# Two neighbouring attention heads on one tile: 64 partitions each, one softmax, one load and store for both

## The chip, the core and the metric

The kernel runs on one core of one Trainium2 chip. TensorE (PE) multiplies and transposes, VectorE (DVE), ScalarE (ACT) and GpSimd (POOL) compute elementwise, and SyncE (SP) issues most of the DMAs. The time is the device time of one launch in microseconds (us). The span in a profile runs from the first to the last instruction and is somewhat shorter.

## The reference

One decoding step, forward and backward. An attention block with 32 heads reads one token x (640 wide) and a cache of 4096 keys and values per head, each 128 wide. A dense block with the Mish activation (640 to 1728 to 640) reads another token, a constant. A sigmoid gate g of x mixes the two:

```python
q = (x @ wq).reshape(B, Sq, H, Dh).transpose(0, 2, 1, 3)
scores = jnp.einsum("bhqd,bhkd->bhqk", q, k_cache) * (Dh ** -0.5)
p = _softmax(scores, axis=-1)
o = jnp.einsum("bhqk,bhkd->bhqd", p, v_cache)
a = o.transpose(0, 2, 1, 3).reshape(B, Sq, H * Dh) @ wo
out = g * a + (1 - g) * b
```

The kernel returns the output and the gradients by x, both caches, wq, wo, w1, b1, w2 and the gate's weights. Inputs and outputs are bfloat16. For each head the gradients of the caches are outer products over the 4096 positions: dV = p times the row dO, and dK = ds times the row q, where ds = p (dO.v - sum of p dO.v). Each cache and each cache gradient has 33.5 MB, so nearly all bytes are those of the four: 134 MB of the 164.56 MB that the DMA engines move.

## The kernel before

**Tiling.** A head's K is one tile Kn of 128 partitions with J = 32 positions on each, 128 values a position: 8 KB on a partition, contiguous in memory, 1 MB in all. V, dK and dV lie the same way. Heads go in groups of G = 4, which share the rows q and dO and the columns of wq and rows of wo that belong to them. The pool kv_in holds four K and four V tiles, outs four output tiles.

**One head, in steps** (names of the helpers and of the tiles in the profile):

- `load_k`, `load_v`: one DMA each, issued by SP.
- `k_pe(h, c)`, `v_pe(h, c)`, c from 0 to 3 (line 541): four transposes on TensorE into one PSUM tile tr (three buffers). `ev` (line 550): ScalarE copies the oldest tr into T.
- `k_rows`, `v_rows` (line 564): eight matmuls each, scores q.k and products dO.v, all into one PSUM tile rw. `rw_cp` (line 575): ScalarE copies rw. `x_tr` (line 581): four transposes bring them to positions on partitions, tile x; two columns of it are the scores and the products.
- `maxes` (lines 587, 589): largest score of each partition. `softmax` (lines 593, 595): a transpose and a maximum give the largest of all. `exps` (line 601): ScalarE's exponential with its sum. `pjs` (line 605), `zd_mm` (line 609): the two sums, over the partitions by a matmul with ones. `probs` (lines 613 to 619): p and ds, each value four times beside itself.
- `dq_o` (line 657): 16 matmuls of ds and p with K and V, into rw again; they are the last readers of the head's K and V. `dqo_red` (line 665) adds up their diagonals one head later.
- `dv_out(h, k)`, `dk_out(h, k)`, k = 0 and 1 (line 624): VectorE writes an outer product of half a tile; after the second half SP stores the tile (line 642).

**Order.** The order of every engine's instructions is that in which the helpers are called: the kernel's pools run under a manual schedule, and each engine takes its instructions in order. The loop over heads at line 772 interleaves head h's softmax with the transposes of head h + 1 and the first two K tiles of head h + 2. The load of head h + 4 is called after dq_o(h), because it takes that head's buffer; thus a load is called two heads before its first transpose:

```python
k_pe(h + 2, 0)
dq_o(h)
v_rows(h + 1)
rw_cp(h + 1)
```

**Between the heads.** At the first head of a group (hh = 0) the previous group's gradients are finished: `f_diag`, `f_bc`, `l_pe`, `f_dwo` (dwo, on ScalarE), and `f_dx` with `f_dwq` (lines 392, 402, five column chunks, on VectorE), two chunks there and three at hh = 1. The next group's rows are made over hh = 1 to 3: `w_pe` (transposes of wo), `g_q`, `g_do`, and `g_qcol`, `g_qpair`, `g_qpair_cp` and their dO counterparts, which bring q and dO into the columns of qz and doz. The dense block's work waits in the list mq and is called in portions by `mlp_some(budget)`, whose costs are the numbers in m_cost (line 674); `dw2_some` adds ScalarE's dw2 copies.

Of the kernel before, what the change touches and what calls it, by code (L numbers as in the profile page):

```python
# [16 lines left out]
def kernel(  # L17
# [24 lines left out]
    nc = tc.nc  # L42
# [5 lines left out]
    J = Sk // P  # L48
# [16 lines left out]
    NTB = J // TB  # L65
    JH = J // 2

    Kv = A_k_cache.rearrange("b h (p j) d -> (b h) p j d", p=P)
    Vv = A_v_cache.rearrange("b h (p j) d -> (b h) p j d", p=P)
    dKv = out_2.rearrange("b h (p j) d -> (b h) p j d", p=P)  # L70
    dVv = out_3.rearrange("b h (p j) d -> (b h) p j d", p=P)
# [20 lines left out]
    KBUFS, VBUFS = 4, 4  # L92
    kv_in = ctx.enter_context(tc.tile_pool(name="kv_in", bufs=KBUFS))
    kvT = ctx.enter_context(tc.tile_pool(name="kvT", bufs=1))
    outs = ctx.enter_context(tc.tile_pool(name="outs", bufs=4))
# [10 lines left out]
    def load_k(h):  # L106
        if h < H:
            kts[h] = kv_in.tile([P, J, Dh], BF16, name="Kn", tag="Kn")
            nc.sync.dma_start(kts[h][:], Kv[h])

    def load_v(h):
        if h < H:
            vts[h] = kv_in.tile([P, J, Dh], BF16, name="Vn", tag="Vn", bufs=VBUFS)
            nc.sync.dma_start(vts[h][:], Vv[h])
# [24 lines left out]
    load_k(0)  # L139
    load_wqp(0)  # L140
    load_wo(0)
    load_v(0)
    load_k(1)
    load_v(1)
    load_k(2)
    load_wo(1)
    load_v(2)
    load_k(3)
    load_v(3)
    w1_sb = const.tile([P, RC, F], BF16, name="w1_sb")  # L150
    nc.sync.dma_start(w1_sb[:], w1_v)
    w2_sb = const.tile([P, FCN, D], BF16, name="w2_sb")
# [17 lines left out]
    nc.vector.reduce_sum(half[:], ident_bf[:].rearrange("p (a k) -> p a k", a=2), axis=AX.X)  # L170
    unzip = const.tile([P, 2, P], BF16, name="unzip")
# [45 lines left out]
    p4b, ds4b = [], []  # L217
    qz = const.tile([P, G, 2, 2, 16], BF16, name="qz")
    doz = const.tile([P, G, 2, 2, 16], BF16, name="doz")
    nc.gpsimd.memset(qz[:], 0.0)  # L220
    nc.gpsimd.memset(doz[:], 0.0)
    for i in range(3):
        for lst, nm in ((p4b, "p4"), (ds4b, "ds4")):
            lst.append(const.tile([P, J * 4], BF16, name=f"{nm}{i}"))
            nc.gpsimd.memset(lst[-1][:], 0.0)
# [3 lines left out]
    def g_new(g):  # L229
        groups[g] = dict(  # L230
            q_row=grp_sb.tile([P, GD], BF16, name="q_row", tag="q_row", bufs=1),
            qs_row=grp_sb.tile([P, GD], BF16, name="qs_row", tag="qs_row"),
            do_row=grp_sb.tile([P, GD], BF16, name="do_row", tag="do_row"),
            dqo=grp_sb.tile([P, 2, G], F32, name="dqo", tag="dqo"),
        )

    def g_q(g):
        gp = groups[g]
        ps = grp([P, GD], F32, "q_ps")
        for rc in range(RC):  # L240
            nc.tensor.matmul(ps[:], lhsT=x_col_bf[:, rc:rc + 1].to_broadcast([P, P]),  # L241
                             rhs=wqs[g][:, rc, :], start=(rc == 0), stop=(rc == RC - 1))
        nc.scalar.copy(gp["q_row"][:], ps[:])
# [5 lines left out]
    def col_mm(row):  # L249
        ps = grp([P, G], F32, "col_ps")  # L250
        for hh in range(G):
            nc.tensor.matmul(ps[:, hh:hh + 1], lhsT=row[0:1, hh * Dh:(hh + 1) * Dh], rhs=ones_bf[0:1, 0:1],
                             start=True, stop=True)
        col = small.tile([P, G], BF16, name="col", tag="col", bufs=2)
        nc.vector.tensor_copy(col[:], ps[:])
        return col
# [7 lines left out]
    def pair_cp(z, ps, at):  # L264
        for par in range(2):
            nc.vector.tensor_tensor(z[:, :, par, :, at],
                                    ps[:, par, :].unsqueeze(2).to_broadcast([P, G, 2]),
                                    half[:].unsqueeze(1).to_broadcast([P, G, 2]), ALU.mult)
# [7 lines left out]
    def g_qpair_cp(g):  # L276
        pair_cp(qz, groups[g].pop("pair"), 4)
# [7 lines left out]
    def g_dopair_cp(g):  # L285
        pair_cp(doz, groups[g].pop("pair"), 5)

    def g_do(g):
        gp = groups[g]
        ps = grp([P, GD], F32, "do_ps")  # L290
        T = wT.pop(("o", g))
        for c in range(RC):
            nc.tensor.matmul(ps[:], lhsT=da_col[:, c:c + 1].to_broadcast([P, P]),  # L293
                             rhs=T[:, c * G:(c + 1) * G, :].rearrange("p t k -> p (t k)"),
                             start=(c == 0), stop=(c == RC - 1))
# [235 lines left out]
    KT, VT, dgms, es, zds, p4s, ds4s = {}, {}, {}, {}, {}, {}, {}  # L531
# [3 lines left out]
    rw_sb, xs, sd = {}, {}, {}  # L535

    def tr_pe(h, tiles, T, c):
        tp = tr_ps.tile([P, TB // 2, P], F32, name="tr", tag="tr")
        words = tiles[h][:, c * TB:(c + 1) * TB, :].rearrange("p a b -> p (a b)").bitcast(F32)
        for t in range(TB // 2):  # L540
            nc.tensor.transpose(tp[:, t, :], words[:, t * P:(t + 1) * P], ident_f[:])  # L541
        trq.append(lambda: kv_ev(tp, T, h, c))

    def ev():
        trq.pop(0)()

    def kv_ev(tp, T, h, c):
        if c == 0:
            T[h] = kvT.tile([P, J // 2, P], F32, name="T", tag="T")
        nc.scalar.copy(T[h][:, (3 - c) * (TB // 2):(4 - c) * (TB // 2), :], tp[:])  # L550

    def k_pe(h, c):
        if h < H:
            tr_pe(h, kts, KT, c)

    def v_pe(h, c):
        if h < H:
            tr_pe(h, vts, VT, c)

    def rows_mm(T, z, first):  # L560
        Tb = T[:].rearrange("p k r -> p (k r)").bitcast(BF16).rearrange("p (t c r a) -> p c a t r", t=4, c=4, a=2)
        for par in range(2):
            for c in range(4):
                nc.tensor.matmul(rw[32 * c:32 * (c + 1), :], lhsT=z[:, par, :, :].rearrange("p m u -> p (m u)"),  # L564
                                 rhs=Tb[:, c, par, :, :], start=first and par == 0, stop=not first and par == 1)

    def k_rows(h):
        rows_mm(KT.pop(h), qz[:, h % G], True)

    def v_rows(h):  # L570
        rows_mm(VT.pop(h), doz[:, h % G], False)

    def rw_cp(h):
        rw_sb[h] = small.tile([P, 4, P], F32, name="rw_sb", tag="rw_sb", bufs=1)
        nc.scalar.copy(rw_sb[h][:].rearrange("p t r -> p (t r)"), rw[:])  # L575

    def x_tr(h):
        t = rw_sb.pop(h)
        xs[h] = s_ps.tile([P, 4, P], F32, name="x", tag="x")
        for j in range(4):  # L580
            nc.tensor.transpose(xs[h][:, 3 - j, :], t[:, j, :], ident_f[:])  # L581
        v = xs[h][:].rearrange("p t r -> p (t r)").rearrange("p (j u) -> p j u", u=16)
        sd[h] = (v[:, :, 4], v[:, :, 5])

    def maxes(h):
        m32 = small.tile([P, 1], F32, name="m32", tag="m32")
        nc.vector.tensor_reduce(m32[:], sd[h][0], axis=AX.X, op=ALU.max)
        dgms[h] = small.tile([P, 1], F32, name="m_s", tag="m_s")
        nc.vector.tensor_scalar(dgms[h][:], m32[:], scale, None, ALU.mult)  # L589

    def softmax(h):
        mx = s_ps.tile([P, P + 2], F32, name="mx", tag="mx")
        nc.tensor.transpose(mx[:, 0:P], dgms.pop(h)[:].to_broadcast([P, P]), ident_f[:])  # L593
        negM = small.tile([P, 1], F32, name="negM", tag="negM")
        nc.vector.tensor_reduce(negM[:], mx[:, 0:P], axis=AX.X, op=ALU.max, negate=True)
        return mx, negM

    def exps(h, negM):
        es[h] = small.tile([P, J], BF16, name="e_bf", tag="e_bf")
        zds[h] = small.tile([P, 2], F32, name="zd", tag="zd")  # L600
        nc.scalar.activation(es[h][:], sd[h][0], ACT.Exp, bias=negM[:], scale=scale, accum_out=zds[h][:, 0:1])  # L601

    def pjs(h):
        pj = small.tile([P, J], F32, name="pj", tag="pj", bufs=2)
        nc.vector.scalar_tensor_tensor(pj[:], in0=sd[h][1], scalar=1.0, in1=es[h][:],  # L605
                                       op0=ALU.mult, op1=ALU.mult, accum_out=zds[h][:, 1:2])

    def zd_mm(h, mx):
        nc.tensor.matmul(mx[:, P:P + 2], lhsT=ones_f[:], rhs=zds[h][:], start=True, stop=True)  # L609

    def probs(h, mx):
# [4 lines left out]
        p4s[h] = p4b[h % 3][:, 0:J * 4].rearrange("p (j t) -> p j t", t=4)  # L616
        nc.vector.tensor_scalar(p4s[h], es.pop(h)[:].unsqueeze(2).to_broadcast([P, J, 4]), rz[:], None, ALU.mult)
        ds4s[h] = ds4b[h % 3][:, 0:J * 4].rearrange("p (j t) -> p j t", t=4)
        nc.vector.scalar_tensor_tensor(ds4s[h], in0=sd.pop(h)[1].unsqueeze(2).to_broadcast([P, J, 4]),  # L619
                                       scalar=negD[:], in1=p4s[h], op0=ALU.add, op1=ALU.mult)  # L620
        zds.pop(h)
# [9 lines left out]
    def out_half(w, h, dst, col4, row, k):  # L631
        hh = h % G
        if k == 0:
            if w == "k" and H - KBUFS <= h < H - 1:
                o_t[w, h] = kv_in.tile([P, J, Dh], BF16, name="Kn", tag="Kn")
            elif w == "v" and h > H - VBUFS:
                o_t[w, h] = kv_in.tile([P, J, Dh], BF16, name="Vn", tag="Vn", bufs=VBUFS)
            else:
                o_t[w, h] = outs.tile([P, J, Dh], BF16, name="o_sb", tag="o_sb")
        outer(o_t[w, h], col4, row[:, hh * Dh:(hh + 1) * Dh], k * JH, (k + 1) * JH)  # L640
        if k == 1:
# [339 lines left out]
```

## Time and profile before

| | |
|---|---|
| median of 3 runs | 401.09 us (400.48 to 402.11) |
| profiled execution | 399.99 us |
| its span | 398.3 us |
| bytes moved | 164.56 MB, 82.44 MB read and 82.44 MB written |
| heads' transfers | 64 loads and 64 stores of 1024 KB |
| median from issue to landing, K load | 16.6 us |
| TensorE clock granted, mean | 0.937 |

The page's first part gives the busy time of the engines, its second the share in 40 slices of the span, the fourth the chain of work that ended last. A row of the waits names the waiting instruction, what released it, the total in us, how often, and the longest. A row of the timeline gives the start, the duration, the engine, the line, the operation with its tiles, and in brackets the idle time before it. For DMA the digits are the mean busy share of 16 engines in tenths.

### The profile page before, as it was taken

To read this page: it belongs to the slowest core of one execution; us is meant where nothing else is said; L and a number is where in the kernel's file an instruction comes from. 1 tells how busy PE (TensorE), PEld (TensorE's weight loads), DVE (VectorE), ACT (ScalarE), POOL (GpSimd) and SP (SyncE) were. 2 spreads that over 40 slices of the span, in tenths; PEclk is the share of its full clock that TensorE was granted. 3 is DMA by queue.
4 is the path that set the end of the run, shared out by engine and by line. 5 is a ranking of instruction groups with operands and counts; after the bars stand their busy time and mean duration, and the time that the engine had idled before them with its cause. 6 is when DMAs were issued, how large, how long until landed. Compare 5 with 4: busy or idle time off the path is not lost.

```text
span 398.3 us, 7758 instructions
## 1 busy us (share of the span) xinstructions
PE 298.7 (75%) x2950; PEld 201.4 (51%) x2950; DVE 288.6 (72%) x823; ACT 232.8 (58%) x468; POOL 29.3 (7%) x54
## 2 busy tenths in 40 slices
PE   2779979777898984875887876968786888578550
PEld 1556647554565663554564553645454555356320
DVE  3216647969688875778898974697897987488880
ACT  2356756853677562763567677575777666285420
POOL 9300023000000000000000070000000000010001
PEclk9999999998999998999999999869999999698955
DMA  7999999999999999999999999999999999999996
GB/s 270 421 426 406 426 419 423 420 418 425 423 423 425 413 408 428 425 415 425 423 423 425 421 424 421 426 412 425 425 423 427 421 427 418 423 432 421 386 419 267
DMA packets 28469, 164.56 MB, mean 413 GB/s; under 512 B 3383, under 2 KB 3384, under 8 KB 11832
## 3 DMA queue, kind: packets, MB, share of 16 engines
q1 hardware_dynamic: 27312, 159.62, 96.6%
q0 software_dynamic: 1088, 4.44, 2.7%
q8 instruction: 23, 0.38, 0.4%
q14 instruction: 14, 0.11, 0.1%
q10 hardware_dynamic: 32, 0.01, 0.0%
HBM read 82.44 MB, written 82.44 MB: 414 GB/s over the span
## 4 chain that ended last, share of the span: by engine, by line
DMA 46%; DVE 25%; PE 20%; ACT 5%; issue 2%; POOL 0%; POOLq 0%; SPq 0%; DVEq 0%; ACTq 0%
DMA out_dram<-o_sb 44%; DVE o_sb L624 10%; PE tr L541 7%; DVE junk L392 4%; PE rw L657 3%; PE rw L564 2%; DVE wq_p L402 2%; DMA wq_p<-in_A_wq_dram 2%; PE x L581 1%; ACT rw_sb L575 1%; ACT do_row L296 1%; PE do_ps L293 1%; PE tr L354 1%; PE h_ps L436 1%; PE q_ps L241 1%
## 5 line engine op out<-in xcount | busy, mean ns | idle before, releaser
L550 ACT COPY T<-tr 128x512 f32<-128x512 f32 x256 | 138.0, 595 | 53.8 <-PE tr L541 38.8
L624 DVE TENSOR_TENSOR o_sb<-qs_row,ds 128x2048 bf16<-128x2048 bf16 x58 | 70.8, 1221 | 37.5 <-DMA out_dram<-o_sb 37.5
L541 PE MATMUL tr<-ident_f,Kn 128*128 128x128 f32 x512 | 84.3, 292 | 5.8 <-DMA Kn<-in_A_k_cache_dram 5.8
L541 PE MATMUL tr<-ident_f,Vn 128*128 128x128 f32 x512 | 82.7, 294 | 7.2 <-ACT T L550 6.4
L541 PEld LDWEIGHTS tr<-ident_f,Vn 128*128 128x128 f32 x512 | 61.4, 151 | 26.9 <-PE tr L541 11.5
L541 PEld LDWEIGHTS tr<-ident_f,Kn 128*128 128x128 f32 x512 | 60.5, 148 | 23.2 <-PE rw L657 13.5
L624 DVE TENSOR_TENSOR o_sb<-do_row,p 128x2048 bf16<-128x2048 bf16 x58 | 68.9, 1229 | 0.0
L575 ACT COPY rw_sb<-rw 128x512 f32<-128x512 f32 x33 | 19.3, 586 | 48.3 <-PE rw L564 46.1
L657 PE MATMUL rw<-Kn,ds 128*4 128x512 bf16 x256 | 36.2, 408 | 4.1 <-DVE ds L619 3.8
L657 PE MATMUL rw<-Vn,p 128*4 128x512 bf16 x256 | 36.2, 408 | 0.0
L593 PE MATMUL mx<-ident_f,m_s 128*128 128x128 f32 x32 | 10.2, 318 | 30.8 <-DVE m_s L589 30.7
L581 PE MATMUL x<-ident_f,rw_sb 128*128 128x128 f32 x132 | 22.1, 291 | 4.6 <-ACT rw_sb L575 1.4
L392 DVE SCALAR_TENSOR_TENSOR junk<-wq_p,dq_bc 128x512 bf16<-128x512 bf16 x35 | 23.9, 683 | 0.0
L609 PE MATMUL mx<-zd,ones_f 128*128 128x2 f32 x64 | 10.7, 237 | 17.6 <-DVE pj L605 17.5
L601 ACT ACTIVATE e_bf<-x,negM 128x32 bf16<-128x32 f32 x32 | 9.4, 293 | 23.0 <-DVE dqo L665 23.0
L593 PEld LDWEIGHTS mx<-ident_f,m_s 128*128 128x128 f32 x32 | 4.4, 139 | 35.2 <-DVE m_s L589 35.2
L410 ACT ACTIVATE wo_g<-da_bc,o 128x640 bf16<-128x640 bf16 x28 | 20.9, 818 | 1.0 <-PE ax_ps L380 1.0
L564 PE MATMUL rw<-T,qz 128*32 128x512 bf16 x256 | 21.4, 412 | 0.0
L581 PEld LDWEIGHTS x<-ident_f,rw_sb 128*128 128x128 f32 x132 | 14.1, 143 | 13.4 <-ACT rw_sb L575 13.4
L564 PE MATMUL rw<-T,doz 128*32 128x512 bf16 x256 | 20.3, 392 | 0.8 <-ACT T L550 0.8
L609 PEld LDWEIGHTS mx<-zd,ones_f 128*128 128x128 f32 x64 | 10.1, 198 | 20.9 <-DVE pj L605 18.2
L657 PEld LDWEIGHTS <-ds 128*4 128x4 bf16 x256 | 9.2, 86 | 20.1 <-DVE ds L619 9.3
(181 smaller groups left out, 381.5 us busy)
## 6 DMA issues: line engine op xcount, KB each, us to landing
out_dram<-o_sb SPq DMA_DIRECT2D x58, 1024.0 KB, 16.4
Kn<-in_A_k_cache_dram SPq DMA_DIRECT2D x32, 1024.0 KB, 16.6
Vn<-in_A_v_cache_dram SPq DMA_DIRECT2D x32, 1024.0 KB, 18.1
wq_p<-in_A_wq_dram SPq DMA_DIRECT2D x4, 1280.0 KB, 14.2
wo_g<-in_A_wo_dram SPq DMA_DIRECT2D x8, 640.0 KB, 17.3
out_dram<-wo_g SPq DMA_DIRECT2D x8, 640.0 KB, 16.5
out_dram<-wq_p SPq DMA_DIRECT2D x4, 1280.0 KB, 9.5
out_dram<-Kn SPq DMA_DIRECT2D x3, 1024.0 KB, 7.8
```

Source lines behind the costliest of these rows:

```text
L392: nc.vector.scalar_tensor_tensor(jq[:], in0=wqs[g][:, c, :], scalar=1.0, in1=groups[g]["dq_bc"][:], op0=ALU.mult, op1=ALU.mult, accum_out= ...
L410: nc.scalar.activation(wos[g][:, hh, :], da_bc[:], ACT.Copy, scale=groups[g]["o4"][:, hh:hh + 1])
L541: nc.tensor.transpose(tp[:, t, :], words[:, t * P:(t + 1) * P], ident_f[:])
L550: nc.scalar.copy(T[h][:, (3 - c) * (TB // 2):(4 - c) * (TB // 2), :], tp[:])
L564: nc.tensor.matmul(rw[32 * c:32 * (c + 1), :], lhsT=z[:, par, :, :].rearrange("p m u -> p (m u)"), rhs=Tb[:, c, par, :, :], start=first an ...
L575: nc.scalar.copy(rw_sb[h][:].rearrange("p t r -> p (t r)"), rw[:])
L581: nc.tensor.transpose(xs[h][:, 3 - j, :], t[:, j, :], ident_f[:])
L593: nc.tensor.transpose(mx[:, 0:P], dgms.pop(h)[:].to_broadcast([P, P]), ident_f[:])
L601: nc.scalar.activation(es[h][:], sd[h][0], ACT.Exp, bias=negM[:], scale=scale, accum_out=zds[h][:, 0:1])
L609: nc.tensor.matmul(mx[:, P:P + 2], lhsT=ones_f[:], rhs=zds[h][:], start=True, stop=True)
L624: nc.vector.tensor_tensor(dst[:, a:b, :].rearrange("p j (k t) -> p j k t", t=4), row.rearrange("p (k t) -> p k t", t=4).unsqueeze(1).to_br ...
L657: nc.tensor.matmul(rw[32 * c:32 * c + 4, :], lhsT=c4[:, 4 * jb:4 * jb + 16].rearrange("p (j t) -> p t j", t=4)[:, 0, :], rhs=N[:, jb:jb + ...
```

## The change

Two neighbouring heads become one pair; 16 pairs take the place of 32 heads, and a group has two pairs. The first head of a pair lies on partitions 0 to 63, the second on 64 to 127, and each partition holds J = 64 positions, 16 KB. Both heads' tiles are contiguous in memory, so a pair's K is one DMA of 2 MB. The pools keep their bytes: two K pairs, two V pairs, two output tiles.

Scores of both heads pass through one rw tile (each pair's T has two halves, which take different columns of qz and doz, so each pair calls `k_rows` and `v_rows` twice) and one x tile. A new step `sels` copies the right columns for each half of the partitions from x into a tile sd, on ScalarE. The maximum is taken per half, the sums over a half by the block matrix blk_f, and dq_o takes its weights from two new masked tiles, dsm and pm, so that each head's partitions go to its own rows. Outer products are in quarters of a tile. The first and the last pair are loaded (pair 0) and stored (both) in halves.

The loop runs over pairs. load_k(i + 2) is called after dq_o(i), and k_pe(i + 2, 0) and (i + 2, 1) stand at the end of the same iteration. f_dx and f_dwq come all five at the end of the first pair's iteration, together with g_q, g_qcol, w_pe and g_do of the next group. mlp_some is called with other budgets. The opening loads are put in another order, with two wq and three wo tiles.

```diff
-    J = Sk // P
+    J = 2 * Sk // P
+    JU = J // 2
+    NP = H // 2
+    HP = P // 2
...
+    Kv, Vv, dKv, dVv = [t.rearrange("b (i a) (q j) d -> (b i) (a q) j d", a=2, j=J)
+                        for t in (A_k_cache, A_v_cache, out_2, out_3)]
...
-    KBUFS, VBUFS = 4, 4
+    KBUFS, VBUFS = 2, 2
...
-    outs = ctx.enter_context(tc.tile_pool(name="outs", bufs=4))
+    outs = ctx.enter_context(tc.tile_pool(name="outs", bufs=2))
...
+    def sels(i):
+        v = xs[i][:].rearrange("p t r -> p (t r)").rearrange("p (j u) -> p j u", u=16)
+        sd[i] = small.tile([P, 2, J], F32, name="sd", tag="sd", bufs=1)
+        for a in range(2):
+            hs = slice(a * HP, (a + 1) * HP)
+            nc.scalar.copy(sd[i][hs].rearrange("p s (k j) -> p k s j", k=2),
+                           v[hs, :, 8 + 4 * a:12 + 4 * a].rearrange("p j (k s) -> p k s j", k=2))
...
+    def zd_mm(i, mx):
+        nc.tensor.matmul(mx[:, P:P + 2], lhsT=blk_f[:], rhs=zds[i][:], start=True, stop=True)
...
+        for m, c4 in ((dsmb, ds4s), (pmb, p4s)):
+            nc.vector.tensor_tensor(m[:], c4[i][:, :, 0:2], half[:].unsqueeze(1).to_broadcast([P, J, 2]),
+                                    ALU.mult)
...
-    for h in range(H - 1):
+    for i in range(NP - 1):
...
+        probs(i, mx)
...
+        dv_out(i, 0)
+        dv_out(i, 1)
+        v_pe(i + 1, 0)
+        v_pe(i + 1, 1)
+        k_rows(i + 1, 1)
+        ev()
+        ev()
+        dq_o(i)
+        load_k(i + 2)
+        load_v(i + 2)
+        v_pe(i + 1, 2)
+        ev()
+        v_pe(i + 1, 3)
+        ev()
+        dv_out(i, 2)
+        dv_out(i, 3)
...
+        v_pe(i + 1, 4)
+        v_pe(i + 1, 5)
+        v_rows(i + 1, 0)
+        ev()
+        ev()
...
+        dk_out(i, 0)
...
+        v_pe(i + 1, 6)
+        ev()
+        v_pe(i + 1, 7)
+        ev()
+        k_pe(i + 2, 0)
+        v_rows(i + 1, 1)
+        rw_cp(i + 1)
+        if i + 2 < NP:
+            ev()
+        dk_out(i, 1)
+        x_tr(i + 1)
+        sels(i + 1)
+        maxes(i + 1)
+        k_pe(i + 2, 1)
...
+        if hp == 0:
             if nx:
                 g_new(g + 1)
+                g_q(g + 1)
+                g_qcol(g + 1)
             if pv:
                 l_pe(g - 1, 0, G)
                 l_add(g - 1, g - 1, True)
                 for t in range(G):
                     f_dwo(g - 1, t)
                 f_dwo_st(g - 1)
+                for c in range(RC):
                     f_dx(g - 1, c)
                     f_dwq(g - 1, c)
                 f_dwq_st(g - 1)
...
+        if i >= 1:
+            mlp_some(0.9 if hp == 0 else 4.5)
             dw2_some(2)
```

## The prediction

> **What bounds the kernel now.** I read parts 1, 2, 4 and 6 of the page, then the waits, then the timeline of the first head. Durations come from the one profiled execution: span 398.3 us, 399.99 us with the 1.7 us around it; the median of the runs, 401.09, is 1.1 us above it.
>
> ```profile
> span 398.3 us, 7758 instructions
> PE 298.7 (75%) x2950; PEld 201.4 (51%) x2950; DVE 288.6 (72%) x823; ACT 232.8 (58%) x468; POOL 29.3 (7%) x54
> DMA  7999999999999999999999999999999999999996
> DMA packets 28469, 164.56 MB, mean 413 GB/s; under 512 B 3383, under 2 KB 3384, under 8 KB 11832
> DMA 46%; DVE 25%; PE 20%; ACT 5%; issue 2%; POOL 0%; POOLq 0%; SPq 0%; DVEq 0%; ACTq 0%
> ```
>
> No engine is above 75%, but the 16 DMA engines are full in every slice but the first and last: bytes bound this kernel, 164.56 MB at about 422 GB/s. The compute waits for them, and only where output tiles come free:
>
> ```profile
> DVE o_sb L624 <- DMA out_dram<-o_sb: 37.5, 20, 4.7
> ...
> PE tr L541 <- DMA Kn<-in_A_k_cache_dram: 5.8, 1, 5.8
> ...
> Kn<-in_A_k_cache_dram SPq DMA_DIRECT2D x32, 1024.0 KB, 16.6
> ```
>
> The second line matters: TensorE waited for a K tile once, at the very start. A load takes 16.6 us in the full queue, but it is issued two heads before its first transpose, so this costs nothing.
>
> The first head gives the durations of a chain that nothing slows:
>
> ```profile
> 0.81 0.38 SPq L109 DMA_DIRECT2D Kn<-in_A_k_cache_dram  x1
> 5.80 1.94 PE L541 MATMUL tr<-ident_f,Kn 128*128 128x128 f32 x8 [5.80 <-DMA Kn<-in_A_k_cache_dram]
> 26.66 0.63 PE L564 MATMUL rw<-T,doz 128*32 128x512 bf16 x8 [0.81 <-ACT T L550]
> 27.34 0.59 ACT L575 COPY rw_sb<-rw 128x512 f32<-128x512 f32 x1 [0.73 <-PE rw L564]
> 27.98 0.66 PE L581 MATMUL x<-ident_f,rw_sb 128*128 128x128 f32 x4
> 28.90 0.15 DVE L589 TENSOR_SCALAR m_s<-m 128x1 f32<-128x1 f32 x1
> 33.23 2.35 DVE L624 TENSOR_TENSOR o_sb<-do_row,p 128x2048 bf16<-128x2048 bf16 x2
> 34.23 0.62 PE L564 MATMUL rw<-T,doz 128*32 128x512 bf16 x8
> ```
>
> 1 MB lands 5.0 us after its issue with an empty queue, of which its 8 packets an engine take 2.5 (309 ns each, the median in the trace's packet records): 2.5 us is latency. From the last score rows to the end of m_s are 2.4 us. The 16 matmuls of dq_o stand between 33.37 and 34.4.
>
> **The change part by part.** *Transfers.* The bytes stay. K, V, dK and dV rows become 16 KB: 128 transfers become 70, 16384 packets of 8 KB become 8192. Packets of 2048, 8192 and 20480 bytes took 84, 309 and 761 ns: 9 ns each beyond their bytes. That is 8192 x 9 / 16 = 4.6 us of DMA time, and 0.5 us for the 928 completion packets that go with 58 transfers. Lower bound nothing, if rows are cut at 8 KB, upper 5.1. I take 5, but it is on the path only if DMA stays the bound.
>
> *Small operations.* Per pair one m, m_s, pj, rz, negD and exp fall away (184, 153, 183, 164, 218, 293 ns) and one rw_cp (586); added are two sels on ScalarE (nearest: 266 ns for 128x128 from PSUM) and the masks dsm and pm (nearest: o_sel, 286 ns). VectorE gains about 16 us of 288.6 in all, ScalarE about 20 with the halved q_row and do_row copies, TensorE about 15 (x_tr and mx at half the number). All of this counts only where the chain below passes through it, and there it is counted.
>
> *The load that moved.* KBUFS goes from 4 heads to 2 pairs, so load_k(i+2) can be issued only after dq_o(i), and its first transpose, k_pe(i+2,0), stands in the same iteration, ahead of v_rows(i+1,1), rw_cp, x_tr and the whole softmax of pair i+1. TensorE runs in order. So there is now a loop, from the end of dq_o(i) to the end of dq_o(i+1):
> - load_k: wake and latency 2.7, 8 packets an engine of 609 ns (two of 309 less 9) 4.9: 7.6 us. The store of dk(i-1) was issued some 4.6 us earlier and is through by then; it adds nothing. Meanwhile TensorE has six V tiles and one set of rows, about 3.8 us (0.52 us an eviction): it waits about 4 us in every iteration. Bounds: 7.0 and 8.5.
> - k tile 0.5; rows to m_s 2.4; sels 0.6: 3.5 us.
> - VectorE from m_s to the masks, in program order (next to next in the timeline): mx 0.6, negM 0.35, dqo 0.15, dk_out 2 and 3 at 1.14, pj 0.15, f_diag 0.9, probs 1.55 with masks: 6.0 us where i is odd. Where i is even: 2.5 until l_add (g_q, q_row, col and l_pe, one after the other), f_dx and f_dwq five times 0.99, the pair copies 0.6, no f_diag: 12.8 us.
> - dq_o: twice 1.05 and the hand-over: 2.25.
>
> Sum: 19.35 us odd, 26.15 even. Before, f_dx and g_q were spread over four heads, and nothing tied them to a load. Seven of each: 318.5 us. Corrections: the first even loop has no f_dx, -2.6; the load of K pair 2 stands behind the rest of the opening loads (17.4 MB, until about 45 us), +7; the MLP work that mlp_some puts on VectorE between m_s and the masks (dh 0.81 each, dx 0.98, dw1 0.6, act, bc): +26.5, of which 18 at odd ends, where the budget is 4.5. Together 349 us for 14 loops, 25 on average.
>
> At one place a page prices the load: the Trainium skill, page "DMA: Bandwidth & Descriptors", section "Anatomy of one DMA", gives a fixed 2.0 us and bytes / 436 GB/s for a transfer by the GpSimd path, an estimate of 6.8 us here. By it the sum would be 14 x 0.8 = 11 us less; the first load of this trace, on the path that is used, has 2.5 us beside its packets, and I keep that.
>
> *Other queues.* On SP the loads pass the dv stores, which then follow them; nothing waits for this, as the next dv tile is needed a loop later. wo and wq loads, w1 stores and on POOL the dw2 store move to other iterations, off the loop. The output tiles hold as many bytes as before; dk(i-1) lands about when dk_out(i,0) wants its tile, at most 1 us on VectorE, which is idle there.
>
> *Start.* dq_o(0) ended at 34.4. Added: six evictions 3.1, sels 0.6, masks 0.75, a longer dq_o 1.05, less 0.65 of do_row: about 39 us.
>
> *End.* From dq_o(14), without a load: 7.2 us to m_s, f_dx 5, softmax and dk(14) 5.5, then eight outer products of 1.15 with the last group's pieces: 28.2 us to the end of dk_out(15,3). In the old profile that point is 384.4, 13.9 before the end; the work behind it hardly changes.
>
> Sum: 39 + 349.4 + 28.2 + 13.9 = 430.5 us of span, 432 with the 1.7; it stands against 399.99 us, and a median may lie 1 us above it.
>
> **The rivals.** *A: DMA stays the bound, the kernel gets faster.* A loop moves 8.39 MB of heads and on average 1.31 MB of weights: 23.0 us at 422 GB/s, 22.7 with fewer packets. If my loops average 25 only on paper and are really under 22.7, the queue never empties. Then the time is 399.99 - 5, plus 0 to 4 us for an end whose output comes in larger pieces: 395 to 399. For it: the first heads of the old trace ran 7.8 us each, and VectorE is at 72%. Against it: three rows would each have to be 10% shorter. A page speaks for it: the same page of the Trainium skill, section "Why small descriptors are slow", has about 3 cycles a packet beside 32 bytes a cycle, so half the packets save an estimated 2 us of DMA time. By that rule, the trace (9 ns) agrees in sign. Chance 0.10, with a third of it within 0.5%.
>
> *B: the forecast, the load exposed*, 406 to 452: 0.78.
>
> *C: worse.* VectorE also waits for the dk tile on the path, or ScalarE's f_dwo and dw2 copies (3.3 and 1.6 us) delay exp in the even loops: +1.5 to 3 us a loop, 453 to 475. ScalarE at 58% speaks against it. Chance 0.08. What is left, 0.04, lies between A and B at 400 to 406.
>
> **How the numbers follow.** B's low end: load 7.0 and VectorE rows overlapping by 0.7 more a loop, plus a start 3 us earlier: 432 - 14 x 1.6 - 3 = 406. High end: load 8.5 and 0.5 us of ScalarE a loop: 432 + 20 = 452. A measurement of this kernel tells about 0.5% from no change (the runs spread by 0.4%). Faster: two thirds of A, 0.07. Same: 0.05 (the rest of A, a part of the gap). Slower: 0.88. The range 406 to 452 leaves out A, C and the gap, about 2 in 10.
>
> **What would show it.** The waits should have TensorE at the K transposes waiting for the DMA of Kn about 14 times, some 4 us each, where there was one; the row of VectorE waiting for stores should shrink to little; DMA digits should fall to 8, and GB/s to about 380; packets under 8 KB stay near 10900 while the total falls by some 9100. Loads should land in about 8 to 10 us instead of 16.6. VectorE's share falls to about 64%. I am wrong if the Kn wait is absent or below 1 us a pair, if the DMA row stays at 9, or if even loops take no longer than odd ones.

## The result, and the profile after

The changed kernel takes 483.35 us (median of 4 runs, 481.33 to 486.63), the kernel before 401.17 (400.48 to 402.11): a ratio of 1.206, 95% interval 1.202 to 1.210. The forecast was 432 with a range of 406 to 452. The direction is right, the time lies 31 us above the range, and the loss is 82 us where 31 were expected.

Lines of parts 1, 2, 4 and 6 of the page of the changed kernel. In the two rows of digits each digit is one fortieth of the span, in tenths.

```profile
span 482.2 us, 7409 instructions
PE 333.6 (69%) x2886; PEld 231.9 (48%) x2886; DVE 279.9 (58%) x728; ACT 225.0 (47%) x452; POOL 27.1 (6%) x50
PEclk9779598886979658685776758688596675959665
DMA  8999948896699959998498788999569697998997
DMA packets 20114, 164.53 MB, mean 341 GB/s; under 512 B 2455, under 2 KB 2456, under 8 KB 10904
PE 38%; DMA 34%; DVE 16%; ACT 8%; issue 2%; POOL 0%; POOLq 0%; SPq 0%; ACTq 0%
...
Kn<-in_A_k_cache_dram SPq DMA_DIRECT2D x15, 2048.0 KB, 8.7
```

The row of DMA digits, 9 all along before, now has holes down to 4: in each of the even loops there are 1.9 to 6.5 us in which no packet moves. No engine is busier than 69%. VectorE and ScalarE did lose work, if less than costed (8.7 us where I had 16, 7.8 where I had 20). TensorE has fewer instructions and yet 333.6 us of work instead of 298.7, and the clock row says why: a mean granted clock of 0.754, where it was 0.937 with this row:

```profile
PEclk9999999998999998999999999869999999698955
```

The waits of the changed kernel (engine, line waited for, releaser: us in total, times, longest):

```profile
DVE m L604 <- ACT sd L599: 121.1, 16, 12.4
...
PE tr L549 <- DMA Kn<-in_A_k_cache_dram: 79.4, 16, 8.6
...
DVE o_sb L645 <- DMA out_dram<-o_sb: 8.2, 5, 2.6
```

The wait that was forecast is there: TensorE stands before the K transposes for 79.4 us (8.1 of them at the start, 71.3 in the 14 loops), where it was 5.8; VectorE's waits for stores, 37.5 us before, are 8.2; and VectorE stands for 121 us before the score row, behind the load. To see what that wait does, here is one loop (from the end of dq_o(6) to the end of dq_o(7), i = 6, an even one), first in the timeline (start, duration, engine, line):

```profile
208.50 0.33 SPq L110 DMA_DIRECT2D Kn<-in_A_k_cache_dram  x1
...
218.81 1.09 PE L549 MATMUL tr<-ident_f,Kn 128*128 128x128 f32 x4 [6.44 <-DMA Kn<-in_A_k_cache_dram]
219.82 1.04 PE L575 MATMUL rw<-T,doz 128*32 128x512 bf16 x8
...
221.56 1.11 PE L592 MATMUL x<-ident_f,rw_sb 128*128 128x128 f32 x4 [0.69 <-ACT rw_sb L586]
...
223.53 0.15 DVE L606 TENSOR_SCALAR m_s<-m 128x1 f32<-128x1 f32 x1
...
226.12 2.98 ACT L418 ACTIVATE wo_g<-da_bc,o 128x640 bf16<-128x640 bf16 x4 [0.76 <-PE ax_ps L388]
...
229.01 1.32 ACT L368 COPY wT<-tr 128x512 f32<-128x512 f32 x3
...
229.62 2.03 PE L301 MATMUL do_ps<-wT,da_col 128*64 128x256 bf16 x10 [1.25 <-ACT wT L368]
...
231.29 0.24 DVE L272 TENSOR_TENSOR qz<-pair_ps,half 128x8 bf16<-128x8 f32 x2
...
232.50 0.42 PE L610 MATMUL mx<-ident_f,m_s 128*128 128x128 f32 x1
...
238.89 0.28 DVE L641 TENSOR_TENSOR pm<-p,half 128x128 bf16<-128x128 bf16 x1
```

and then by stretches, the odd loop before it (i = 5) and this one, each cut at the end of dq_o, the first K transpose, m_s and the masks (us; busy time of PE, PEld (TensorE's weight loads), DVE, ACT and POOL, each with its instructions; then granted clock, DMA share, GB/s):

```profile
184.20:192.00 7.80, 3.89 (x48) 2.99 (x48) 4.91 (x6) 3.13 (x6) 0.00 (x0) 0.88 0.98 370
192.00:196.90 4.90, 4.17 (x32) 2.90 (x33) 0.37 (x3) 1.70 (x5) 0.00 (x0) 0.50 0.99 354
196.90:206.50 9.60, 7.79 (x64) 6.19 (x63) 9.19 (x31) 4.70 (x10) 0.00 (x0) 0.82 1.01 415
206.50:208.50 2.00, 2.00 (x41) 0.78 (x32) 1.97 (x5) 1.08 (x2) 0.00 (x0) 1.00 1.06 438
208.50:218.80 10.30, 3.71 (x32) 2.60 (x33) 5.98 (x7) 3.13 (x6) 0.00 (x0) 0.77 1.01 424
218.80:223.70 4.90, 4.20 (x23) 2.60 (x24) 0.37 (x2) 1.73 (x5) 0.00 (x0) 0.50 1.01 378
223.70:239.20 15.50, 13.40 (x121) 10.46 (x119) 11.86 (x41) 9.74 (x19) 0.00 (x0) 0.65 0.42 175
239.20:241.10 1.90, 1.90 (x33) 0.76 (x31) 1.90 (x2) 0.66 (x2) 0.00 (x0) 1.00 0.97 414
```

Three things are to be read from it. The stretch right behind the wait runs at a granted clock of exactly 0.50 in both loops: four transposes of x take 1.11 us, where the first head of the kernel before had 0.66. The stretch before it is 10.3 us in the even loop and 7.8 in the odd one, of which TensorE waits 6.4 and 3.9; the DMA engines are full in both. And in the long third stretch of the even loop the DMA engines are busy 42% of the time: both pairs of buffers are held, and there is nothing to move.

The 14 loops cut in the same way, from the trace's instructions, against the forecast:

| us, 14 loops | forecast | measured | more |
|---|---|---|---|
| dq_o to the first K transpose ("load 7.6") | 113.4 | 126.4 | 13.0 |
| K transpose to m_s ("k tile ... m_s ... 3.5") | 49.0 | 68.2 | 19.2 |
| m_s to the masks (VectorE) | 155.5 | 167.7 | 12.2 |
| masks to the end of dq_o | 31.5 | 33.6 | 2.1 |
| start, until the end of dq_o(0) | 39 | 42.2 | 3.2 |
| end, from the end of dq_o(14) | 42.1 | 44.1 | 2.0 |
| span | 430.5 | 482.2 | 51.7 |

The odd loops have 24.9 us in the mean (forecast 21.9), the even ones 31.7 (28.0).

### The profile page after: what moved, and what is told of

Its sections match the earlier page's. It is cut to its first block, busy times and chain, and to the rows that moved or that the text cites. A ratio compares the mean times of both kernels' runs of the same rounds, so it can differ in the third digit from the quotient of the medians.

```text
span 482.2 us, 7409 instructions
## 1 busy us (share of the span) xinstructions
PE 333.6 (69%) x2886; PEld 231.9 (48%) x2886; DVE 279.9 (58%) x728; ACT 225.0 (47%) x452; POOL 27.1 (6%) x50
## 2 busy tenths in 40 slices
DMA packets 20114, 164.53 MB, mean 341 GB/s; under 512 B 2455, under 2 KB 2456, under 8 KB 10904
## 4 chain that ended last, share of the span: by engine, by line
PE 38%; DMA 34%; DVE 16%; ACT 8%; issue 2%; POOL 0%; POOLq 0%; SPq 0%; ACTq 0%
DMA Kn<-in_A_k_cache_dram 32%; PE tr L549 15%; PE rw L681 6%; PE rw L575 5%; DVE o_sb L645 5%; ACT wo_g L418 4%; PE x L592 4%; PE do_ps L301 3%; DMA out_dram<-Kn 2%; PE q_ps L246 2%; DVE junk L508 2%; ACT rw_sb L586 2%; DVE mjunk L529 1%; DVE junk L310 1%; ACT wT L368 1%
## 5 line engine op out<-in xcount | busy, mean ns | idle before, releaser
L549 PE MATMUL tr<-ident_f,Kn 128*128 128x128 f32 x512 | 107.9, 368 | 80.4 <-DMA Kn<-in_A_k_cache_dram 79.4
L549 PEld LDWEIGHTS tr<-ident_f,Kn 128*128 128x128 f32 x512 | 85.2, 194 | 97.4 <-issue 85.9
L549 PE MATMUL tr<-ident_f,Vn 128*128 128x128 f32 x512 | 71.3, 284 | 2.1 <-ACT T L560 2.1
L549 PEld LDWEIGHTS tr<-ident_f,Vn 128*128 128x128 f32 x512 | 56.6, 143 | 21.9 <-ACT T L560 6.4
L586 ACT COPY rw_sb<-rw 128x512 f32<-128x512 f32 x17 | 9.9, 585 | 92.1 <-PE rw L575 87.5
L681 PE MATMUL rw<-Kn,dsm 128*8 128x512 bf16 x256 | 34.0, 413 | 3.2 <-DVE dsm L641 3.1
L681 PE MATMUL rw<-Vn,pm 128*8 128x512 bf16 x256 | 34.1, 413 | 0.0
L575 PE MATMUL rw<-T,doz 128*32 128x512 bf16 x256 | 26.5, 499 | 0.8 <-ACT T L560 0.8
L301 PE MATMUL do_ps<-wT,da_col 128*64 128x256 bf16 x80 | 14.7, 377 | 9.7 <-ACT wT L368 9.6
L681 PEld LDWEIGHTS <-dsm 128*8 128x8 bf16 x256 | 11.8, 92 | 17.1 <-DVE dsm L641 6.1
L301 PEld LDWEIGHTS <-da_col 128*64 128x64 bf16 x80 | 10.0, 143 | 12.8 <-issue 10.5
```

The costliest lines, as they stand in the source:

```text
L301: nc.tensor.matmul(ps[a * HP:(a + 1) * HP, :], lhsT=da_col[:, c:c + 1].to_broadcast([P, HP]), rhs=T[:, c * G:(c + 1) * G, :].rearrange("p ...
L575: nc.tensor.matmul(rw[32 * c:32 * (c + 1), :], lhsT=z[:, at:at + 32], rhs=Tb[:, c, par, :, :], start=first and par == 0, stop=last and par ...
L586: nc.scalar.copy(rw_sb[i][:].rearrange("p t r -> p (t r)"), rw[:])
L681: nc.tensor.matmul(rw[32 * c:32 * c + 8, :], lhsT=m[:, jb:jb + 4, :].rearrange("p q a -> p (q a)"), rhs=N[:, jb:jb + 4, :].rearrange("p j ...
```

## The experiments

Ratios are to the kernel before, whose medians beside these kernels were 401.55 to 401.96 us. Times of loops come from each one's profiled execution, and the line numbers in a fence are those of its own kernel.

### Keeping TensorE busy in the wait

```
+        if i + 2 < NP:
+            for _ in range(24):          # 42 in the second kernel
+                nc.tensor.matmul(mx[:, 2 * P:4 * P], lhsT=ident_bf[:], rhs=da_bc[:, 0:2 * P], ...)
         k_pe(i + 2, 0)
```

> The changed kernel with 24 idle bf16 matmuls (128x256, into unused columns of mx) on TensorE ahead of k_pe(i+2, 0), where it waits 3.5 to 8.8 us for the K load in each of 14 loops; nothing else differs, the extra matmuls feed nothing. Theory 'clock': the wait costs more than its own length, because TensorE comes out of it at half the granted clock. Then the granted clock rises from 0.75 to over 0.85, the stretch from the K tile to m_s shrinks from 4.9 us to 3.5 to 3.8, and the even loops' g_q and w_pe work runs faster: 1.3 us x 14 and 1 us x 7 less, 483 becomes 455 to 462. Rival 'only the load': the clock falls where nothing waits, and the time stays at 478 to 488.

Measured: 477.3 us, ratio 1.189 (1.182 to 1.196), 6 us less than the changed kernel and just under the rival's range. The mechanism is there, the amount is not: the mean granted clock rose to 0.834, not over 0.85. In nine loops, with 0.7 to 3.0 us of the wait left behind the fillers, K transpose to m_s took 3.5 to 4.0 us; in the other five, with 2.9 to 5.9 left, it stayed at 4.87. That is 9.3 us less in all. But the loads then took 3.2 us more; that this is because the loop they belong to had become shorter and the queue had not, is likely, but not shown.

> As the first filler kernel, with 42 idle matmuls instead of 24 ahead of k_pe(i+2, 0): 24 took 2.6 us of a mean wait of 5.2, and the stretch from the K tile to m_s stayed at half clock where 3 us or more of the wait were left, and ran in 3.6 us where less than 2 were. 42 take 4.5 us. Theory 'clock, in full': the stretch falls to 3.6 us in at least 12 of 14 loops (50 us in all instead of 60.4 with 24 and 68.6 with none), and the time from 477 to 466 to 472. Rival 'the queue takes it back': what a loop gains the next load loses, as 3.5 us of the first filler's gain went, and the time stays at 474 to 480, because the transfers of the odd loops do not come sooner.

Measured: 469.5 us, ratio 1.166 (1.157 to 1.174). K transpose to m_s took 3.52 to 3.55 us in 12 of the 14 loops, at a granted clock of 1.00, and 52.2 us in all (68.2 without fillers); the load took 133.1 us (126.4). Two lines of its page, the clock by fortieths and the x transposes (busy us, mean ns of one), and the x transposes of the kernel before:

```profile
PEclk9899769998898959979798888998699897998555
...
L592 PE MATMUL x<-ident_f,rw_sb 128*128 128x128 f32 x68 | 12.1, 304 | 11.7 <-ACT rw_sb L586 11.7
```
```profile
L581 PE MATMUL x<-ident_f,rw_sb 128*128 128x128 f32 x132 | 22.1, 291 | 4.6 <-ACT rw_sb L575 1.4
```

One x transpose takes 304 ns in the mean, where it was 416 in the changed kernel and 291 before. By the clock records TensorE spent 52 us at half clock in the kernel before, 240 in the changed one, 160 with 24 fillers, 126 with 42. So at least 14 us of the 82 are the price of the clock alone, won back by matmuls that compute nothing; the theory had the right range here.

### Taking the load off the path

```
-        k_pe(i + 1, 2)
-        ev()
         mx, negM = softmax(i)
+        for c in range(3):
+            k_pe(i + 1, c)
+            ev()
 ...
-        k_pe(i + 2, 0)
         v_rows(i + 1, 1)
 ...
-        k_pe(i + 2, 1)
```

> The changed kernel with k_pe(i+2, 0) and k_pe(i+2, 1) taken out of iteration i and put behind the softmax transpose of iteration i+1, so that v_rows(i+1, 1), rw_cp and x_tr no longer stand behind the K load on TensorE. Theory 'load on the path': the wait of 3.5 to 8.8 us (mean 5.2) and the half clock behind it leave all 14 loops, some 6 us each, less 1.1 us for two more evictions between mx and zd_mm: 483 - 70 = 413, down to a floor near 400 where DMA binds again; 400 to 420. Rival 'the wait only moves': K lands 9.4 us after dq_o while m_s would then be ready at 7.3 or so, TensorE waits for K behind mx instead and zd_mm stands behind it; only half is won, 440 to 460.

Measured: 420.5 us, ratio 1.050 (1.045 to 1.055). That is 0.5 us above the range of "load on the path". 63 of the 82 us come back, by nothing but the place of three K tiles (two from the iteration before, and the one that stood ahead of the softmax transpose) and their evictions; the 14 loops fall from 395.9 to 330.6. Two lines of its waits and one of its page:

```profile
DVE o_sb L645 <- DMA out_dram<-o_sb: 45.6, 18, 5.6
...
PE tr L549 <- DMA Kn<-in_A_k_cache_dram: 11.8, 5, 6.2
```
```profile
DMA  7999999998699999999999999999799999989997
```

The digits are 9 again nearly throughout, and VectorE waits for stores as it did before the change: DMA is the bound. The wait for K did move behind mx in four loops, as the rival had it, but with 5.6 us in all; the other 6.2 are the first K tile of the kernel.

### A shorter load

```
-        return list(load(kts, Kv, "Kn", i))
+        return list(load(kts, Kv, "Kn", i, 2))     # two DMAs of 8 KB rows
```

> The changed kernel with each K load of a pair (2 MB) in two halves of 8 KB rows, so that k_pe(i+2, 0) and the three tiles after it wait for the first half alone. Theory 'the load's length is on the path': the first half lands 2.5 us (8 packets of 309 ns an engine) earlier, the wait falls from 5.2 to 2.8 us and in part of the loops the clock stays up (1.3 us each): 14 x 2.5 and 7 x 1.3, 483 becomes 437 to 445. Rival 'the queue takes half of it back': the odd loops' transfers then end later against the loop, 455 to 468. Rival 'latency and queue, not length': 475 or more.

Measured: 451.6 us, ratio 1.123 (1.118 to 1.128). The waits say

```profile
PE tr L549 <- DMA Kn<-in_A_k_cache_dram: 50.0, 14, 6.5
```

29 us less than 79.4, and the time fell by 32. In the loops with odd i the load fell from 59.3 to 41.4 us, 2.6 each, the length of half a load; in the seven with even i from 67.1 to 59.7 only. In three of these it hardly moved (9.1, 9.1 and 10.3 us for 9.0, 9.5 and 10.0): the DMA engines were full there when the load was issued, with the pair before. The mechanism is that of the rival "the queue takes half of it back"; the time lies between the two ranges, 3.4 us under the rival's.

### The store ahead of the load

```
-        dk_out(i - 1, 2)   # behind exps
-        dk_out(i - 1, 3)   # behind pjs
 ...
-        dk_out(i, 1)
+        for k in range(1, 4):
+            dk_out(i, k)
```

> The changed kernel with dk_out(i, 2) and dk_out(i, 3) done behind dk_out(i, 1) in the same iteration instead of in the next one's softmax: the 2 MB store of dk then goes out while TensorE waits for K, not 4 us ahead of the K load. Theory 'store ahead of the load': the K load took 9.4 us from dq_o to the first transpose instead of my 7.6 because that store was still in the queue; it falls to 7.6 to 8, 1.6 us x 14, and two outer products of 1.2 leave the stretch from negM to the masks, 2.4 us x 14: 483 becomes 425 to 432. Rival 'load long by itself': the load stays at 9.4 and only VectorE's share is won, 445 to 452. Rival 'TensorE and ScalarE set that stretch': 470 or more.

Measured: 467.2 us, ratio 1.163 (1.158 to 1.167), between the two rivals. The load did not get shorter in all (130.1 us for 126.4); m_s to the masks fell by 14.2, of which 9.3 in the odd loops. The loads of this kernel tell what my 7.6 us are. In six loops the DMA engines had stood idle at the issue (share 0.03 or less in the 2 us before); in five of them, as at 128.6 and 182.8 us of the span, the K tile came 7.65 to 7.97 us after dq_o. In the sixth, at 346.8, it took 9.96, and why is open. Where the engines were full throughout (at 149.4), it took 9.50. So 7.6 is about the price in an empty queue, and a pair's transfers leave no empty queue behind a short odd loop: 8.39 MB and a wo load fill 21.4 us at 422 GB/s, and the loop that ended at 149.4 lasted 20.8.

### The group's work in the even loops

First f_dx and f_dwq alone into the odd iterations:

```
-                for c in range(RC):
-                    f_dx(g - 1, c)
-                    f_dwq(g - 1, c)
-                f_dwq_st(g - 1)
 ...
         dk_out(i, 1)
+        if hp == 1 and pv:        # the same four lines
+            f_in(g - 1)
```

> The changed kernel with the five f_dx and f_dwq of a group taken from behind m_s in the even iterations and put behind dk_out(i, 1) of the odd ones, where VectorE waits for the K load (the last group keeps its place). Theory of the prediction: VectorE's chain sets the even loops, six loops lose 5.0 us each, 483 becomes 451 to 457. Rival 'ScalarE': f_dwo's four copies (2.98 us) hold up the wT evictions, so g_do and the mx transpose behind it were only 0.64 us later than VectorE in the loop I looked at; moving f_dx wins at most 1 us a loop, 475 to 483.

Measured: 499.7 us, ratio 1.237 (1.227 to 1.247): slower by 16, outside both. Two things were learned. m_s to negM in the even loops stayed at 9.6 to 10.2 us (9.7 to 11.0 before the move), so five f_dx and five f_dwq less on VectorE bought next to nothing there; what sets it lies on TensorE and ScalarE, as the next kernel bears out. And two loops grew from 32.6 to 39.8 and 39.4. A line of SyncE's waits and its issues around one of them:

```profile
SPq L129 <- DMA out_dram<-wq_p: 25.7, 2, 14.8
```
```profile
209.40 0.38 SPq L129 DMA_DIRECT2D wq_p<-in_A_wq_dram  x1
209.83 1.00 SPq L673 DMA_DIRECT2D out_dram<-o_sb  x1
210.95 0.56 SPq L110 DMA_DIRECT2D Kn<-in_A_k_cache_dram  x1
```

The later wq store made the wq load wait 14.8 us on SP for its buffer, and behind it stood dk's store and then the K load of the loop. The K load went out only 1.5 us after dq_o, but right behind the 3.4 MB that had been held up; TensorE waited 13.7 us for K.

Then f_dwo as well, with f_dx and f_dwq early enough for the wq store:

```
         load_v(i + 2)
+        if hp == 1 and pv:
+            f_in(g - 1)
 ...
+        if hp == 1 and pv:
+            for t in range(G): f_dwo(g - 1, t)
+            f_dwo_st(g - 1)
+            if g + 2 < NG: load_wo(g + 2)
         k_pe(i + 2, 0)
```

> The changed kernel with both parts of a finished group's work taken out of the even iterations: f_dx and f_dwq stand right behind the loads of the odd iteration, f_dwo's four ScalarE copies behind the last V tile there, both in the K load's shadow and early enough that the wq store is through before the next wq load (the last group keeps its place). Theory 'ScalarE and TensorE chain': moving f_dx alone left m_s to negM at 9.7 us in the even loops, because wT and g_do wait behind f_dwo; with both gone it falls to what the first even loop shows without them, 6.1 us: 3.5 us x 6, 483 becomes 460 to 466. Rival 'the DMA queue takes it back': loops shorter than the transfers of one pair push the next K load back, half of it is lost, 470 to 478.

Measured: 492.5 us, ratio 1.225 (1.219 to 1.231), again outside both. m_s to the masks fell from 95.5 to 77.2 us in the six even loops that had the work, 3.0 each, where the last kernel had 92.8, so ScalarE's f_dwo was part of what set it. That gain was lost again, and more, in the same way as in the last kernel, this time at the wo load:

```profile
SPq L133 <- DMA out_dram<-wo_g: 70.3, 5, 16.6
```

Two loops lasted 40.2 and 39.1 us. The gain of a clean move is therefore not shown by a time, only by this stretch.

### Depth, with single heads

```
-    KBUFS, VBUFS = 4, 4        # kernel before
+    KBUFS, VBUFS = 3, 3
 ...     # among the opening loads
-    load_k(3)
-    load_v(3)
```

> The kernel before with 3 K and V buffers of one head instead of 4: the load of head h+3 is issued after dq_o(h), two heads ahead, which is as many bytes ahead as the changed kernel's one pair; its first transpose, k_pe(h+3, 0), stands in the next iteration ahead of dq_o(h+1). Theory 'order': what costs is not the depth but that the K tile is wanted in the same iteration, ahead of the score rows; here it is wanted an iteration later, the DMA queue stays full, and the time is 400 to 410. Rival 'depth': with a head less in flight the queue runs empty and TensorE waits for K in most heads, 425 to 470.

Measured: 430.4 us, ratio 1.074 (1.067 to 1.080). The theory "order" is wrong here, and the rival has it:

```profile
PE tr L539 <- DMA Kn<-in_A_k_cache_dram: 50.3, 19, 5.8
```

One head less in flight, with single heads and their whole order kept, costs 29 us and brings the same wait in 18 heads (the 19th wait is the first K tile of the kernel). So pairing itself isn't needed for a loss: looking ahead by two heads' bytes instead of three is enough to expose the load. It is not the whole loss either, 29 of 82 us. Three buffers of a pair were not tried.

### Versions put together

The K tiles behind softmax and the early dk, by the two diffs shown above:

> The two earlier edits together: the K tiles behind the softmax transpose, and dk_out 2 and 3 behind dk_out 1. With the K tiles moved VectorE waited 45.6 us for output tiles, since the dk store goes out just ahead of the next K and V loads. Theory 'stores late': the store of dk leaves earlier, VectorE's waits shrink, and the 2.4 us of outer products leave the softmax: 420 becomes 406 to 412. Rival 'covered': those waits lie beside the DMA queue that is full anyway, 416 to 423.

Measured: 417.2 us, ratio 1.040 (1.037 to 1.043): the K tiles and dk together, within the range of "covered". VectorE's waits for output tiles fell to 27.9 us, and the time by 3.

The same with half loads, and with exp first on ScalarE:

```
         mx, negM = softmax(i)
+        exps(i, negM)
         for c in range(3):
             k_pe(i + 1, c)
 ...
-        exps(i, negM)
```

> The best order so far (K tiles behind the softmax transpose, dk_out 2 and 3 behind dk_out 1), with the K load in two halves and exp ahead of the K tiles' evictions on ScalarE. There TensorE still waits 1 to 4 us for K behind mx in some loops, and exp stood 0.5 to 3.7 us behind negM. Theory 'compute still sets the even loops': both leave the path, 417 becomes 408 to 413. Rival 'DMA is the bound there': the queue has 17 us of idle time in all, 11 of them at the ends and in the loop with the MLP's activations, and the time stays at 414 to 418.

Measured: 418.8 us, ratio 1.042 (1.037 to 1.047), no gain, and 0.8 us above the rival's range: TensorE's wait for K is 6.0 us, once, at the very start, and 36 of the 40 DMA digits are 9, so DMA binds.

Another kernel wrote the loop anew, in this order, with f_dwo and the wo load in the odd iterations as above:

```
+        mx, negM = softmax(i)
+        exps(i, negM)
 ...     # k_pe(i + 1, 0 to 5) around pjs, zd_mm and probs
+        dq_o(i)
+        load_k(i + 2)
+        load_v(i + 2)
+        for k in range(4):
+            dv_out(i, k)
 ...     # k_pe 6 and 7, V tiles, with dk_out(i, 0 to 3) between them
+        v_rows(i + 1, 1)
 ...     # rw_cp to maxes(i + 1), then the group's block as before
```

> The changed kernel in another order, with all its work: the K tiles of pair i+1 behind the softmax transpose of pair i, exp ahead of their evictions on ScalarE, dq_o(i) and the loads as soon as the masks are ready, the four outer products each of dv(i) and dk(i) behind them, f_dwo in the odd iterations. Theory 'with the load off the path DMA is the bound again': 9.70 MB a loop at 422 GB/s is 23.0 us, 14 of them with 41 us before and 41 behind are 404; 396 to 408. Rival 'even loops stay too long for two buffers': odd loops of 17 us, even ones of 27, the queue runs empty in the even ones as it does with only the K tiles moved: 412 to 422.

Measured: 443.1 us, ratio 1.105 (1.102 to 1.109), above both ranges. Loops of both kinds lasted 21 to 28 us: softmax(i+1) still stands behind the group's and the MLP's work in program order, exp waited 35.8 us for negM, and SP again held K loads behind a wo load (at 135.3 us dq_o ended, at 137.8 the load went out, with the DMA engines at 0.18 between). How the 35 us above the theory divide among these was not measured.

> Three edits together in the changed kernel, whose order on TensorE stays: 24 idle matmuls ahead of k_pe(i+2, 0), the K load in two halves, and dk_out 2 and 3 behind dk_out 1. One by one they gave 6, 32 and 16 us. Theory 'separate terms of one loop' (half clock, length of the load, outer products and the dk store): they add, less 2 us a loop in the odd loops where the fillers are longer than what is left of the wait (some 1 us x 7): 483 - 54 + 7 = 436; 427 to 440. Rival 'one queue behind them all': once the load is short, the transfers of a pair (23 us) set the odd loops and the group's work the even ones (30 us less 2), 445 to 455.

Measured: 439.9 us, ratio 1.097 (1.092 to 1.101), at the top of the first range. These are the fillers, half loads and the early dk, by the diffs above, in the changed kernel's own order. One by one they gave 6, 32 and 16 us, together 43 of these 54: they add for the most part. The wait for K before the fillers' end has all but gone in the odd loops, which have 19.6 us in the mean (24.9); the even ones have 29.9 (31.7).

## Why the prediction was right in direction and wrong in size

**The bound, and rival A.** Right: bytes bound the kernel before, and the change took it from that bound. The saved packet time was there in the small (16 KB packets took 611 ns in the median, two of 309 less 7) and never reached the path. That count itself was a little off: 8355 packets went, not 9100, since the first and last pairs keep rows of 8 KB.

**The loop, and rival B.** Right in its mechanism: one wait for K in every loop, 5.1 us in the mean where "about 4" was said; the kernel that only takes the K tiles out of TensorE's way returns 63 us. B was the case that came, with its terms too small.

**The step that failed first: "k tile 0.5; rows to m_s 2.4; sels 0.6: 3.5 us".** It measured 4.87 us in each of the 14 loops, 19.2 us more in all, the largest of the errors. I took the durations from the first head, at full clock, and placed them behind a wait that I had myself forecast. In this kernel each of the 14 waits before the K tile (3.3 to 8.6 us) is followed by a granted clock of 0.50 up to m_s, and the fillers show cause and price: the stretch falls to 3.55 us, what the forecast said, when TensorE has something to do in the wait. The Trainium skill, page "TensorE: Matmul & The Clock Gate", section "HAM oscillation — how this bites in real kernels", describes just this case, a wait for a DMA in each tile that throttles TensorE anew each time; the trace agrees, with 0.50 behind every one of the 14 waits. The price here was 1.4 us a loop.

**"load_k ... 7.6 us ... The store of dk(i-1) ... is through by then; it adds nothing".** 7.6 is right where little else is still to be moved: in five of the loops (7.61 to 7.99 us) 0.2 to 0.8 MB of other transfers landed between the end of dq_o and the first K transpose. In the other eight behind the first loop it was 1.2 to 2.3 MB, and the term was 8.4 to 10.3 us. Slow packets, of which the last section tells, are not what made those loads long: 16 KB packets took 685 to 702 ns in the mean in the five short loads, and 621 to 636 in the three longest. The term measured 13.0 us more, 15.1 in loops 2 to 14 less 2.1 in the first, for which I had 7 us extra. My upper bound of 8.5 was not wide enough. The reason given was half of it: not dk's store alone, but all that a short odd loop has not yet moved stands before the next load, as the kernel with the early dk store and the one with half loads show. I costed the DMA queue either as the bound (rival A) or as empty (B). In fact the engines were 0.84 to 1.01 busy over the odd loops and 0.73 to 0.83 over the even ones, which have their hole in the long stretch behind m_s.

**"12.8 us" from m_s to the masks in the even loops.** Measured 15.2 in the mean, with MLP work of which I had 1.2: 10.6 us over seven loops, against 1.5 in the odd ones. The sum on VectorE was nearly right (in the loop shown qz is done 7.9 us behind m_s, forecast 8.05), but VectorE didn't set it: f_dwo, wT, g_do and mx on ScalarE and TensorE, partly at half clock, ended 0.64 us behind the last of VectorE's pieces, and taking f_dx away left m_s to negM at 9.6 to 10.2 us. Rival C named ScalarE's f_dwo as a delay of its own kind, to which I gave 0.08. It was there beside B, not instead of it. That the errors of all terms could have one sign and add up, as all four did, is what the range left out: its upper end took 0.9 us a loop for the load and 0.5 for ScalarE, and nothing for the stretch behind the wait.

**Start and end.** 3.2 and 2.0 us more than forecast; small.

**Slips in the sums.** Three sums of the forecast do not come out of their own terms, and none decides the result. The pieces listed for the even loops add up to 13.1 us, not 12.8. The low end takes 1.6 us a loop where its terms give 0.6 and 0.7, so it should be 411 us, not 406. And the rows listed for the small operations give VectorE 5.3 us (16 x 0.902 less 32 x 0.286), not 16; 8.7 were measured.

**"Other queues ... nothing waits for this".** True for the changed kernel: no load in its loops waits on SP for a store of a weight. But two of my own edits show how near it was: a store of a weight a few us later, and SP's order carried the delay into the K load.

**What would show it.** Right: the wait of TensorE before Kn (14 times in the loops), the shrunk waits for stores, 10904 packets under 8 KB, loads landing in 8.7 us, even loops longer than odd. Digits of 8 and 380 GB/s were too good: 4 to 9 and 341.

## What to carry to other kernels

When a change makes a TensorE wait recur, cost the work behind the wait at the slow clock, not with rows from a stretch where TensorE was busy: here that was 1.4 us after each wait of 5. Count a buffer scheme in bytes ahead of the first reader, and look where that reader stands on its in-order engine: three of a pair's 16 tiles moved behind the softmax transpose were worth 63 us, while VectorE's 8.7 us less work did not keep the changed kernel from losing 82. And a queue that is full in one half of a period and has a hole in the other is neither a bound nor free; price a load by what the half before it leaves behind.

## What was not expected of the hardware

The slow clock lasts far longer than the wait. In the loop shown, TensorE's last V transpose ended at 212.4 us, the clock records go to 0.50 at 214.0, work resumes at 218.8, and the clock returns at 234.5, 15.7 us later; in the odd loop before it, from 190.1 to 200.4, 8.3 us after work resumed. Over all 14 loops the clock returned 5.7 to 8.9 us after work resumed in ten, and 14.9 to 15.8 us in four, all four of them even. Until then TensorE's work has no gap above 0.69 us in those ten; in the four it has a further one of 1.25 us for ScalarE. Whether that gap makes the return late was not tried. The same page of the Trainium skill, in its section "Part 1: The HAM clock gate (the "warmup" mystery)", gives about 3.4 us of sustained work for the return; every return here took longer, with work that has gaps.

16 KB packets were slower than their median tells: 660 ns in the mean against 611, 805 of 7424 above 700 ns, 21 us of all 16 engines' time in the run. Summed over the packets, the changed kernel has 414.8 us of transfers an engine, the kernel before 397.6, with the same bytes in 8355 packets more. Of the 805 slow ones 354 started in the first 4 us after the end of dq_o and 415 between 8 and 14 us after it. In the kernel with the K tiles and dk moved the mean is 630. So of the 16.6 us that the span of this best version (414.9 us) still lies above that of the kernel before, 4 are longer packet time (401.8 us) and 11 idle time of the DMA engines (17.5 us, mean of the 16, against 6.7; the changed kernel had 71). Why these packets are slow was not tried and stays open.
